# Loading two small parameter vectors from GpSimd and reading a branch flag at two moments, in a fused attention and rational MLP kernel

## The chip, the cores and the metric

The kernel runs on one core of one Trainium2 chip. The metric is the device time of one execution in microseconds (us). Before the change it is 251.97 us, the median of three runs (251.5 to 252.45).

## The reference

Linear attention with a sketched product kernel is followed by an MLP with a rational activation. Inputs are `q`, `k`, `v` of shape (4, 4, 1088, 32), two sketches `S1`, `S2` (8 x 32), `w_in` (128 x 2048), `w_out` (2048 x 128), and two small vectors `a` (4 values) and `b` (2 values).

```python
def phi(x):
    a = np.einsum('rd,bhsd->bhsr', S1, x)
    b = np.einsum('rd,bhsd->bhsr', S2, x)
    return np.einsum('bhsi,bhsj->bhsij', a, b).reshape(*x.shape[:-1], r * r)
kv = np.einsum('bhsf,bhsd->bhfd', phi(k), v)
num = np.einsum('bhsf,bhfd->bhsd', phi(q), kv)
den = np.einsum('bhsf,bhf->bhs', phi(q), np.sum(phi(k), axis=2))[..., None] + 1e-06
# tokens: (4352, 128), the heads side by side
h = (num / den) @ w_in
P = a[0] + a[1]*h + a[2]*h**2 + a[3]*h**3
Q = 1.0 + np.abs(b[0])*np.abs(h) + np.abs(b[1])*h**2
out = (P / (Q + 1e-06)) @ w_out
```

Note that `P / Q` is a ratio of polynomials in `h`; `b` alone decides which form of it the kernel can use.

## The kernel before

**Two programs behind one branch.** `run` (L123) is built twice: with `Fast`, always executed, and with `General`, executed only if the flag `special` is set (L834 to L837). In this data the flag is 0, so the second body is jumped over. The flag is computed on GpSimd from `b`, and every engine loads it into a register (`flag`, L793) before the compare-and-branch at the end (its instructions carry L836).

**Order of the work.** Nothing is scheduled by a compiler: `ORDER` (L24) is a list of steps `name:index`, and each step issues its instructions in that order, each engine taking its own in sequence. The steps that matter here: `ba` takes the absolute value of `b` on ScalarE (L818) and then runs `fitting` (L757), 14 small instructions on GpSimd that produce the flag and `c_fit`; `bi` runs `factors` (L774), a reciprocal `c_inv` on VectorE (L775) followed by five small GpSimd instructions that make scale factors; `rg` loads some of them into ScalarE registers; `wo` scales `w_out` by the factors; `lq`, `lk`, `lv`, `lw`, `lx` issue loads from SyncE's queue; `st` stores a block of output; `fl` loads the flag; `hi` marks a place for the branch hint.

**The first attention block.** Keys of batch 0 (class `Keys`, L297) come in three parts: `kt` transposes k on VectorE (L315), `ks` multiplies by the sketches on TensorE (L323), `kc` copies one half out of PSUM on ScalarE (L330), `kf` forms the 64 products per row on VectorE (L335, buffer `k_p`), `kp` multiplies them with v on TensorE (L364), `kk` copies the result to `kvz` on ScalarE (L374). Queries of batch 0 come as blocks 0 to 3 (`qt` transpose on VectorE L387 into one of two `qT` buffers, `qs` sketches on TensorE L400 or L473, `qc` copy on ScalarE L407 or L410, `qf` products on VectorE L416 or L419, `qp` TensorE L428, `qd`, `qi`, `qx` denominator, reciprocal and quotient on VectorE L437, L444, L449, `qb` transpose on TensorE L455, `qk` copy on ScalarE L462 into `xT`). Blocks 0 and 1 use columns 0 to 511 of q, which are loaded first; blocks 2 and 3 use the rest, loaded by `lq:0`.

**The MLP.** For 17 units of 4096 columns `h` does the first matmul (L519) in four pieces, `e` copies each to bf16 on ScalarE (L525), further steps on ScalarE and VectorE build three terms, and `G` accumulates them against `w_out` (L677). `st` transposes 256 or 512 columns of the sum on VectorE into `out_sb` (L686) and stores them with four DMAs (L694), all from SyncE, but for the last block, where two of the four come from ScalarE's queue.

**Queues and semaphores.** Loads go out from SyncE and, at the very start, from ScalarE: `s_raw`, two pieces of k, then `a_sb` (L209) and `b_sb` (L211), each broadcast to 128 partitions. Eight semaphores serve the DMAs of these two queues in turn, so a DMA waits until the eighth DMA before it, in program order over both queues, has landed.

GpSimd's own program before the chain of `ba` is: the masks (L229 to L233, from which VectorE makes the sketch matrices at L255), memsets, the identity, and copies `S21` and `SAB` of the sketches (L261, L267).

Of the kernel before, what the change touches and what calls it, by code (L numbers as in the profile page):

```python
# [19 lines left out]
class Fast:  # L20
# [1 line left out]
    R_ON_ACT = (0, 0, 0, 0, 1, 1, 0, 0, 1, 0, 0, 0, 0, 1, 1, 1, 0, 0, 0, 0, 0, 1, 0, 0, 0, 0, 1, 0, 0, 0, 1, 1, 1, 1)  # L22
    TURNS = (11, 0, 0, 0, 2, 0, 0, 0, 0)
    ORDER = """  # L24
tn:4 tn:0 lw:1 lq:0 kt0:0 lw:0 kt1:0 lx:1 kt2:0 lx:0 ks1:0 kt3:0 ks0:0 lk:1 qt:0 ks2:0 kc0:0 kc1:0 kf0:0 kf1:0 qs:0
kc2:0 qt:1 kf2:0 qc:0 kp0:0 ba:0 kp1:0 qf:0 kp2:0 qt:3 qs:1 kk:0 bi:0 qt:2 lq:1 lv:1 qc:1 qf:1 qp:0 qd:0 qs:2 qi:0
qx:0 qb:0 wo:3 qc:2 qk:0 qf:2 wo:0 qp:1 qs:3 qp:2 qd:1 wo:5 wo:1 h2:0 qd:2 wo:4 e2:0 qi:1 h3:0 qx:1 qi:2 h0:0 wo:2
qx:2 qb:1 rg:0 kt0:1 e3:0 e0:0 qb:2 pd1:0 qk:2 h1:0 kt1:1 u1:0 m1:0 lk:2 qk:1 e1:0 qc:3 ks0:1 ks1:1 qt:6 qt:4 h2:1
pd0:0 u0:0 kc0:1 kc1:1 kf0:1 m0:0 kt0:2 ln1:0 h0:1 e2:1 kt1:2 ex1:0 e0:1 v0:0 rd1:0 h1:1 ks1:2 qs:4 kf1:1 h3:1 qt:5
# [24 lines left out]
G1:14 h3:16 m1:14 u0:16 x1:14 ra1:15 ln0:16 e2:16 ex0:16 e3:16 s1:15 u2:16 m1:15 G0:14 u3:16 G5:14 G1:15 G0:15 G3:14  # L54
ra0:16 ln3:16 G2:14 ln2:16 G4:14 G0:16 ex3:16 pd1:15 s0:16 x1:15 G3:15 ex2:16 st:14 m0:16 ra3:16 ra2:16 s3:16 pa0:16
G4:15 G5:15 pa2:16 pa3:16 s2:16 G6:16 hi:0 m3:16 G1:16 G4:16 G2:15 m2:16 G3:16 G7:16 x0:16 st:15 G2:16 x2:16 G5:16
x3:16 G8:16 fl:0 st:16
    """.split()
    W_ENG = (1, 1, 0, 0, 0, 1)
    P_ON_ACT = (0, 0, 0, 0, 0, 0, 0, 0, 0, 0, 0, 0, 0, 0, 0, 0, 0, 0, 0, 0, 0, 0, 0, 0, 0, 0, 0, 0, 0, 0, 0, 0, 1, 1)  # L60
# [62 lines left out]
def run(  # L123
# [13 lines left out]
    nc = tc.nc  # L137
    ctx = ExitStack()
    fast = plan.FAST
# [15 lines left out]
    consts = ctx.enter_context(tc.tile_pool(name="consts", bufs=1))  # L155
# [38 lines left out]
    for i, s_in in enumerate((S1, S2)):  # L194
# [5 lines left out]
                      in_=bass.AP(tensor=k.tensor, offset=k.offset, ap=[[S * D // 32, 128], [W, NM], [1, 4 * D]]))  # L200
    nc.sync.dma_start(out=k0[:, 0:km].rearrange("p (m x) -> p m x", m=NM - 1)[:, :, 4 * D:],
                        in_=k0_src[:, 0:km].rearrange("p (m x) -> p m x", m=NM - 1)[:, :, 4 * D:])
# [3 lines left out]
    nc.sync.dma_start(out=q0[:, 0:512], in_=q0_src[:, 0:512])  # L206
    a_sb = consts.tile([128, 4], FP, name="a_sb")
    b_sb = consts.tile([128, 2], FP, name="b_sb")
    nc.scalar.dma_start(out=a_sb, in_=bass.AP(tensor=moe_a.tensor, offset=moe_a.offset,  # L209
                                              ap=[[0, 128]] + list(moe_a.ap)))  # L210
    nc.scalar.dma_start(out=b_sb, in_=bass.AP(tensor=moe_b.tensor, offset=moe_b.offset,  # L211
                                              ap=[[0, 128]] + list(moe_b.ap)))
    nc.scalar.preload_act_table_set("abs_reciprocal_sqrt_and_small" if fast else "natural_log_exp_and_others")
    load_v(0)
# [7 lines left out]
    def turn(i, cols=512):  # L222
        idle_ps = bank()
        for _ in range(plan.TURNS[i]):
            nc.tensor.matmul(idle_ps[:, :cols], lhsT=idle[:, 0:128], rhs=idle[:, :cols], start=True, stop=True)
# [48 lines left out]
    b_fit, c_fit, c_inv = (consts.tile([128, 2], FP, name=x) for x in ("b_fit", "c_fit", "c_inv"))  # L274
    a_k = consts.tile([128, 3], FP, name="a_k")
    special = consts.tile([128, 1], mybir.dt.int32, name="special")
    k_in_reg, k_sq_reg = (nc.scalar.alloc_register(x) if fast else None for x in ("k_in_reg", "k_sq_reg"))
    a1, a2, a3 = a_sb[:, 1:2], a_sb[:, 2:3], a_sb[:, 3:4]
    a3_reg = nc.scalar.alloc_register("a3_reg" if fast else "a3_reg_g")
# [401 lines left out]
    def store(i):  # L681
        t0, tl, f0, per = units[i]
        if f0 + per < nf:
            return
        o = mid.tile([128, TC], FP, name="out_sb")
        nc.vector.transpose(out=o[:, :tl], in_=outs[t0][:, :tl])  # L686
        c = t0
        while c < t0 + tl:
            b = c // S
            ce = min(t0 + tl, (b + 1) * S)  # L690
            o_b = out[b * S:(b + 1) * S, :].rearrange("(g j) d -> g j d", g=32)
            j0, j1 = (c - b * S) // 32, (ce - b * S) // 32
            for e in range(d_model // 32):
                (nc.scalar if t0 + tl == n_tok and e % 2 else nc.sync).dma_start(  # L694
                    out=o_b[:, j0:j1, e * 32:(e + 1) * 32],
                    in_=o[e * 32:(e + 1) * 32, c - t0:ce - t0].rearrange("p (j d) -> p j d", d=32))
            c = ce
# [8 lines left out]
    def w_part(x):  # L706
        y, f = x // 2, x % 2 * (nf // 2)
        o, t = w_sb[y][:, f:f + nf // 2], w_out_sb_f[:, f:f + nf // 2]
        if fast:
            if plan.W_ENG[x]:  # L710
                nc.scalar.activation(out=o, in_=t, func=ACT.Copy, scale=a_k[:, y:y + 1])
            else:
                nc.vector.tensor_scalar(out=o, in0=t, scalar1=a_k[:, y:y + 1], scalar2=None, op0=AX.mult)
        elif y == 2:
            (nc.scalar.copy if plan.W_ENG[x] else nc.vector.tensor_copy)(out=o, in_=t)
        elif plan.W_ENG[x]:
            nc.scalar.activation(out=o, in_=t, func=ACT.Copy, scale=a_sb[:, y:y + 1])
        else:
            nc.vector.tensor_scalar(out=o, in0=t, scalar1=a_sb[:, y:y + 1], scalar2=None, op0=AX.mult)
# [37 lines left out]
    def fitting():  # L757
        g = nc.gpsimd
        g.tensor_mul(out=sq, in0=ab0, in1=ab0)
        by(lim, ab1, AX.mult, 2.0 ** -10)  # L760
        by(fit, ab1, AX.is_ge, 2.0 ** -20)
        by(b4, ab1, AX.mult, 2.0)
        by(fit, ab1, AX.is_le, 2.0 ** 20, AX.mult, fit)
        by(fit, ab0, AX.is_ge, lim, AX.mult, fit)
        by(fit, b4, AX.is_ge, sq, AX.mult, fit)
        by(lim, fit, AX.mult, -1.0, AX.add, 1.0)
        by(b_fit, b_abs, AX.mult, fit, AX.add, lim)
        by(b4, b_fit[:, 1:2], AX.mult, 4.0)
        g.tensor_mul(out=sq, in0=b_fit[:, 0:1], in1=b_fit[:, 0:1])
        g.tensor_copy(out=special, in_=lim)  # L770
        by(c_fit[:, 1:2], b4, AX.mult, 1.0 + 1e-6, AX.subtract, sq)
        g.tensor_copy(out=c_fit[:, 0:1], in_=b_fit[:, 0:1])
# [12 lines left out]
        if any(plan.P_ON_ACT):  # L785
            nc.scalar.reg_load(a3_reg, a_sb[0:1, 3:4].bitcast(mybir.dt.int32))

    value = []

    def hint():  # L790
        tc.mark_branch_hint_location("special", "LikelyTaken", [mybir.EngineType.PE, mybir.EngineType.DVE, mybir.EngineType.Activation, mybir.EngineType.SP])

    def flag():  # L793
        value.append(nc.values_load(special[0:1, :], min_val=0, max_val=1, skip_runtime_bounds_check_because="a comparison gives 0 or 1"))

    does = {"e": evac, "h": hidden, "u": d_abs, "w": d_w, "y": d_y, "ln": a_square if fast else a_ln, "ex": a_root if fast else a_exp, "ra": a_inv, "rd": d_inv, "pa": a_p, "pd": d_p,
            "s": d_s, "m": d_hs, "v": d_v, "x": d_g, "G": gather}
# [6 lines left out]
    for step in plan.ORDER:  # L804
        name, i = step.split(":")
        i = int(i)
        if name in q_does:
            getattr(blocks[i](), q_does[name])()
        elif name in k_does:
            getattr(keys[i](), k_does[name][0])(*k_does[name][1:])  # L810
        elif name == "wo":
            w_part(i)
        elif name in loads:
            fetched[name, i] = loads[name](i)
        elif name == "tn":
            turn(i)
        elif name == "ba":
            nc.scalar.activation(out=b_abs, in_=b_sb, func=ACT.Abs)  # L818
            if fast:
                fitting()  # L820
            else:
                nc.scalar.reg_load(a3_reg, a_sb[0:1, 3:4].bitcast(mybir.dt.int32))
        elif name in ("bi", "rg", "hi", "fl"):
            {"bi": factors, "rg": registers, "hi": hint, "fl": flag}[name]()
        elif name == "st":
            store(i)
        else:
            does[name[:-1]](i, int(name[-1]))
# [5 lines left out]
def kernel(tc, *args):  # L834
    special = run(tc, Fast, *args)
    with tc.If(special > 0, label="special"):  # L836
        run(tc, General, *args)  # L837
# [30 lines left out]
```

## Time and profile before

| | us |
|---|---|
| median of three runs | 251.97 |
| lowest, highest | 251.5, 252.45 |
| the profiled execution's own time | 251.9 |
| its span, first to last instruction | 250.0 |
| TensorE busy in it | 240.5 |
| VectorE busy | 233.0 |
| ScalarE busy | 227.9 |
| GpSimd busy | 7.5 |

The profile is of one execution. Its engines are called PE (TensorE matmuls), PEld (weight loads), DVE (VectorE), ACT (ScalarE), POOL (GpSimd) and SP (SyncE); a "q" behind a name means the engine's sequencer, which issues DMAs, waits and branches. Times in a row are the start from the span's beginning and the duration, in us. A row may merge several like instructions (x4), and ends with the idle time before it and what ended that wait. The granted TensorE clock was 0.998 over the span.

### The profile page before, as it was taken

What the parts mean: (1) busy time and instruction counts of PE and PEld (TensorE: products, weight loads), DVE (VectorE), ACT (ScalarE), POOL (GpSimd) and SP (SyncE); (2) the same over time, 40 slices, a digit from 0 to 9 for tenths busy, and PEclk for the clock granted to TensorE, in tenths of its full rate; (3) what the DMA queues carried; (4) which work ended last, traced back from release to release, by engine and by line L of the source; (5) the groups of instructions that cost most, each with busy time, mean ns of one, the idle gap of its engine ahead of it and who ended that gap; (6) DMA issues with size and microseconds to landing.
All of it is one profiled execution on the core that took longest, in us unless ns stands there. A gap on an engine that the chain in (4) does not pass through costs nothing.

```text
span 250.0 us, 4083 instructions
## 1 busy us (share of the span) xinstructions
PE 240.5 (96%) x1585; PEld 133.8 (54%) x1585; DVE 233.0 (93%) x233; ACT 227.9 (91%) x217; POOL 7.5 (3%) x43
## 2 busy tenths in 40 slices
PE   7889999999999999999999999999999999999990
PEld 2668546645645455445555344444544467666770
DVE  3776999899999999999999999999999999999990
ACT  2267999999999999999999999999999999999980
POOL 4340000000000000000000000000000000000000
PEclk9999999999999999999999999999999999999999
DMA  5995348464413176210512200030020211020032
GB/s 155 257 387 89 99 121 188 134 156 78 144 27 100 28 202 138 69 45 16 148 22 77 67 3 0 16 102 3 0 42 0 40 25 22 0 37 8 0 49 42
DMA packets 30534, 19.60 MB, mean 78 GB/s; under 512 B 20400, under 2 KB 26672, under 8 KB 30512
## 3 DMA queue, kind: packets, MB, share of 16 engines
q1 hardware_dynamic: 28864, 18.92, 30.4%
q10 hardware_dynamic: 1648, 0.40, 0.9%
q8 instruction: 13, 0.21, 0.4%
q14 instruction: 9, 0.07, 0.1%
HBM read 16.16 MB, written 3.15 MB: 77 GB/s over the span
## 4 chain that ended last, share of the span: by engine, by line
PE 77%; DVE 13%; DMA 3%; issue 3%; SPq 0%; DVEq 0%
PE h_ps L519 42%; PE att_ps L677 23%; PE att_ps L428 4%; DVE g L658 4%; PE att_ps L364 4%; DVE g L647 3%; DVE s L643 2%; DMA k_sb<-in_k_dram 2%; PE att_ps L455 2%; DMA v_sb<-in_v_dram 2%; PE att_ps L473 2%; PE att_ps L323 1%; DVE p L600 1%; DVE r L630 1%; DVE out_sb L686 1%
## 5 line engine op out<-in xcount | busy, mean ns | idle before, releaser
L519 PE MATMUL h_ps<-xT,w_in_sb 128*128 128x512 f32 (+1 forms) x320 | 125.8, 532 | 0.0
L519 PEld LDWEIGHTS h_ps<-xT,w_in_sb 128*128 128x128 f32 x320 | 59.3, 190 | 44.4 <-issue 34.0
L525 ACT CAST hh<-h_ps 128x1024 bf16<-128x1024 f32 x68 | 72.2, 1086 | 2.1 <-PE h_ps L519 1.9
L613 ACT ACTIVATE ln<-u 128x2048 f32<-128x2048 bf16 (+1 forms) x35 | 67.2, 1950 | 0.0
L677 PEld LDWEIGHTS <-w_out 128*128 128x128 bf16 x432 | 41.8, 98 | 46.0 <-issue 16.5
L618 ACT ACTIVATE r<-ln 128x2048 bf16<-128x2048 f32 x22 | 44.0, 2002 | 0.0
L643 DVE TENSOR_TENSOR s<-hh,r 128x4096 bf16<-128x4096 bf16 (+2 forms) x21 | 39.2, 1872 | 0.0
L677 PE MATMUL att_ps<-r,w_out 128*128 128x512 bf16 (+1 forms) x160 | 34.8, 347 | 0.1
L677 PE MATMUL att_ps<-g,w_out 128*128 128x512 bf16 (+1 forms) x160 | 34.4, 347 | 0.0
L647 DVE TENSOR_TENSOR g<-hh,s 128x4096 bf16<-128x4096 bf16 (+2 forms) x16 | 27.8, 1744 | 0.3 <-PE att_ps L677 0.3
L658 DVE TENSOR_TENSOR g<-g,p 128x4096 bf16<-128x4096 bf16 (+2 forms) x15 | 27.7, 1849 | 0.0
L630 DVE TENSOR_TENSOR r<-r 128x2048 bf16<-128x2048 bf16 x22 | 26.5, 1217 | 0.0
L677 PE MATMUL att_ps<-s,w_out 128*128 128x512 bf16 (+1 forms) x112 | 24.5, 349 | 0.4 <-DVE s L643 0.4
L618 ACT ACTIVATE ln<-ln 128x2048 f32<-128x2048 f32 (+1 forms) x13 | 24.4, 1895 | 0.0
L624 ACT ACTIVATE r<-ln 128x2048 bf16<-128x2048 f32 (+1 forms) x13 | 23.7, 1868 | 0.0
L600 DVE TENSOR_SCALAR p<-hh,a_sb 128x4096 bf16<-128x4096 bf16 (+1 forms) x17 | 21.6, 1273 | 0.6 <-ACT hh L525 0.6
L548 DVE TENSOR_SCALAR u<-hh 128x2048 uint16<-128x2048 uint16 (+2 forms) x24 | 21.7, 905 | 0.4 <-ACT hh L525 0.4
L647 DVE TENSOR_TENSOR g<-hh,p 128x2048 bf16<-128x2048 bf16 (+1 forms) x7 | 11.6, 1663 | 0.0
L658 DVE TENSOR_TENSOR g<-g,s 128x2048 bf16<-128x2048 bf16 (+1 forms) x8 | 11.6, 1463 | 0.0
L428 PEld LDWEIGHTS att_ps<-kvz,q_pT 128*64 128x64 f32 x288 | 9.8, 137 | 3.3 <-issue 1.7
L428 PE MATMUL att_ps<-kvz,q_pT 128*64 128x66 f32 x288 | 11.1, 224 | 0.0
L364 PE MATMUL att_ps<-v_sb,k_p 128*64 128x64 f32 (+1 forms) x288 | 9.2, 222 | 1.0 <-DMA v_sb<-in_v_dram 1.0
(79 smaller groups left out, 146.6 us busy)
## 6 DMA issues: line engine op xcount, KB each, us to landing
a_all<-sk_d SPq DMA_DIRECT2D x6, 384.0 KB
b_all<-sk_d SPq DMA_DIRECT2D x12, 192.0 KB
v_sb<-in_v_dram SPq DMA_DIRECT2D x12, 144.0 KB
k_sb<-in_k_dram SPq DMA_DIRECT2D x3, 544.0 KB
q_sb<-in_q_dram SPq DMA_DIRECT2D x3, 544.0 KB
a_all<-sk_d SPq DMA_DIRECT2D x4, 320.0 KB
b_all<-sk_d SPq DMA_DIRECT2D x8, 160.0 KB
w_out_sb_f<-in_moe_w_out_dram SPq DMA_DIRECT2D x2, 512.0 KB
```

The costliest lines, as they stand in the source:

```text
L428: nc.tensor.matmul(self.nd[g * 64:(g + 1) * 64, o:o + 2 * KW], lhsT=self.q_p[:, c, x + g * 64:x + (g + 1) * 64], rhs=kvz[self.b % 2][:, c, ...
L519: nc.tensor.matmul(t[:, x * tl:(x + 1) * tl], lhsT=w_in_sb[:, f * 128:(f + 1) * 128], rhs=xT[:, x_at(t0):x_at(t0) + tl], start=True, stop= ...
L525: nc.scalar.copy(out=live[i]["hh"][:, part * PW:(part + 1) * PW], in_=live[i]["h", part])
L600: nc.vector.tensor_scalar(out=part_of(i, "p", h), in0=hh, scalar1=a3, scalar2=a2, op0=AX.mult, op1=AX.add)
L613: nc.scalar.activation(out=t, in_=live[i]["u"][:, span(h)], func=ACT.Square, scale=k_in_reg, bias=1.0)
L618: nc.scalar.activation(out=t if r_on_act(i, h) else part_of(i, "r", h), in_=t, func=ACT.Abs_reciprocal_sqrt, scale=k_sq_reg, bias=1.0)
L624: nc.scalar.activation(out=part_of(i, "r", h), in_=live[i]["ln", h], func=ACT.Square)
L630: nc.vector.tensor_mul(out=t, in0=t, in1=t)
L643: nc.vector.tensor_mul(out=part_of(i, "s", h), in0=hh, in1=part_of(i, "r", h))
L647: nc.vector.tensor_mul(out=part_of(i, "g", h), in0=hh, in1=part_of(i, "p" if horner(i, first(h)) else "s", h))
L658: nc.vector.tensor_mul(out=g, in0=g, in1=part_of(i, "s" if horner(i, first(h)) else "p", h))
L677: nc.tensor.matmul(outs[t0][:, :tl], lhsT=w_sb[y][:, f0 + x, :], rhs=part_of(i, key, h)[:, c:c + tl], start=done[0] == 0, stop=done[0] == ...
```

## The change

Four edits, all in `run` and `Fast.ORDER`:

- `a_sb` and `b_sb` are loaded from GpSimd's queue, as its first two instructions ahead of the masks, and no longer from ScalarE's.
- `ba:0` moves from behind `kp0:0` to the third place, ahead of all other ScalarE compute. `bi:0` moves from behind `kk:0` to just behind `qf:0`, ahead of `kp2:0 qt:3 qs:1 kk:0 qt:2`.
- `kf2:0` (VectorE, L335) now stands ahead of `qt:1` (VectorE, L387).
- The flag: at `fl:0`, SyncE, ScalarE and GpSimd load it as before. TensorE and VectorE load it at a new last step `fm:0` from a copy, `late_special`, which GpSimd writes after a dummy copy that reads the last `out_sb`, so after the last output transpose.

```diff
-tn:4 tn:0 lw:1 lq:0 kt0:0 lw:0 kt1:0 lx:1 kt2:0 lx:0 ks1:0 kt3:0 ks0:0 lk:1 qt:0 ks2:0 kc0:0 kc1:0 kf0:0 kf1:0 qs:0
-kc2:0 qt:1 kf2:0 qc:0 kp0:0 ba:0 kp1:0 qf:0 kp2:0 qt:3 qs:1 kk:0 bi:0 qt:2 lq:1 lv:1 qc:1 qf:1 qp:0 qd:0 qs:2 qi:0
+tn:4 tn:0 ba:0 lw:1 lq:0 kt0:0 lw:0 kt1:0 lx:1 kt2:0 lx:0 ks1:0 kt3:0 ks0:0 lk:1 qt:0 ks2:0 kc0:0 kc1:0 kf0:0 kf1:0
+qs:0 kc2:0 kf2:0 qt:1 qc:0 kp0:0 kp1:0 qf:0 bi:0 kp2:0 qt:3 qs:1 kk:0 qt:2 lq:1 lv:1 qc:1 qf:1 qp:0 qd:0 qs:2 qi:0
...
-x3:16 G8:16 fl:0 st:16
+x3:16 G8:16 fl:0 st:16 fm:0
...
-    nc.scalar.dma_start(out=a_sb, in_=bass.AP(tensor=moe_a.tensor, offset=moe_a.offset,
+    nc.gpsimd.dma_start(out=a_sb, in_=bass.AP(tensor=moe_a.tensor, offset=moe_a.offset,
...
-    nc.scalar.dma_start(out=b_sb, in_=bass.AP(tensor=moe_b.tensor, offset=moe_b.offset,
+    nc.gpsimd.dma_start(out=b_sb, in_=bass.AP(tensor=moe_b.tensor, offset=moe_b.offset,
...
+    late_special = consts.tile([1, 1], mybir.dt.int32, name="late_special")
...
         o = mid.tile([128, TC], FP, name="out_sb")
+        last_out[:] = [o]
...
-    value = []
+    value, last_out = [], []
+    special_handles = nc.alloc_registers("special") if fast else None
+    special_regs = {h.engine: h for h in special_handles.handles} if fast else None
...
     def flag():
-        value.append(nc.values_load(special[0:1, :], min_val=0, max_val=1, skip_runtime_bounds_check_because="a comparison gives 0 or 1"))
+        for e in (nc.sync, nc.scalar, nc.gpsimd):
+            e.reg_load(special_regs[e.engine], special[0:1, :])
+
+    def late_flag():
+        nc.gpsimd.tensor_copy(out=late_special, in_=last_out[0][0:1, 0:1])
+        nc.gpsimd.tensor_copy(out=late_special, in_=special[0:1, :])
+        for e in (nc.tensor, nc.vector):
+            e.reg_load(special_regs[e.engine], late_special)
+        value.append(nc.snap(special_handles, min_val=0, max_val=1))
```

More of the change, by code (lines that the diff above doesn't have):

```diff
@@ L822, in run @@
                 nc.scalar.reg_load(a3_reg, a_sb[0:1, 3:4].bitcast(mybir.dt.int32))
-        elif name in ("bi", "rg", "hi", "fl"):
-            {"bi": factors, "rg": registers, "hi": hint, "fl": flag}[name]()
+        elif name in ("bi", "rg", "hi", "fl", "fm"):
+            {"bi": factors, "rg": registers, "hi": hint, "fl": flag, "fm": late_flag}[name]()
         elif name == "st":
```

## The prediction

> **What bounds the kernel now.** I read the page first, to see which engine has no room.
>
> ```profile
> PE 240.5 (96%) x1585; PEld 133.8 (54%) x1585; DVE 233.0 (93%) x233; ACT 227.9 (91%) x217; POOL 7.5 (3%) x43
> ```
>
> Three engines are over 90% busy, and none of their instructions is removed except two DMA issues. So the body between some 18 and 240 us can only be shifted, and the change must win or lose at the two ends. The second view is the chain of work that ended last, over the first 35 us (start, duration, what).
>
> ```profile
> 6.03 3.98 DMA v_sb<-in_v_dram
> ...
> 10.26 2.32 PE att_ps L364 x72
> 12.58 1.06 PE h_ps L400 x8
> 13.64 0.64 PE att_ps L428 x16
> ...
> 14.29 0.44 DVE qT L387
> ...
> 15.65 0.43 DVE x_tok L449
> ...
> 18.05 5.38 PE h_ps L519 x24
> ```
>
> The start hangs on a DMA (v lands at 6.03 + 3.98 = 10.01), then on PE, then at 14.29 on DVE, and from 18.05 PE runs the MLP without a gap. The hand-over to DVE is where the change acts. The timeline of DVE shows why it was late:
>
> ```profile
> 14.21 0.17 DVE L775 RECIPROCAL c_inv<-c_fit 128x2 f32<-128x2 f32 x1 [1.05 <-POOL c_fit L772]
> 14.29 0.44 DVE L387 STREAM_TRANSPOSE qT<-q_sb 128x256 f32<-128x256 f32 x1
> 14.66 0.65 DVE L416 TENSOR_TENSOR q_pT<-h_ps,a_all 128x512 f32<-128x512 f32 x1
> ```
>
> DVE sat idle for 1.05 us behind a reciprocal that waits for GpSimd, with a transpose queued behind it that PE needs.
>
> The other end is the timeline of the last store; DVE, ACT and SP have these rows:
>
> ```profile
> 244.14 0.45 DVE L686 STREAM_TRANSPOSE out_sb<-att_ps 128x256 f32<-128x256 f32 x1 [0.69 <-PE att_ps L677]
> ...
> 244.62 0.87 ACTq L694 DMA_DIRECT2D out_dram<-out_sb  x2
> 244.78 0.32 SPq L694 DMA_DIRECT2D out_dram<-out_sb  x1
> ...
> 245.14 2.01 SPq L694 DMA_DIRECT2D out_dram<-out_sb  x1
> ```
>
> Call T the end of the last transpose, 244.59. Four equal stores follow. Three take 0.32 to 0.46 us to issue (two together 0.87 on ACT); the fourth takes 2.01 and ends at 247.15, T + 2.56. The program's closing steps, by the instructions of L836 (duration in ns, first and last start):
>
> ```profile
> L836 SPq EVENT_SEMAPHORE  x8: 17/17/17, 247.8 to 248.6; - x8
> ...
> L836 PEldq COMPARE_BRANCH  x1: 396/396/396, 244.1 to 244.1; - x1
> L836 DVEq COMPARE_BRANCH  x1: 84/84/84, 244.2 to 244.2; - x1
> ...
> L836 ACTq COMPARE_BRANCH  x1: 76/76/76, 245.5 to 245.5; - x1
> L836 SPq COMPARE_BRANCH  x1: 70/70/70, 247.2 to 247.2; - x1
> ```
>
> SP branches when its fourth issue is done (247.2), clears eight semaphores until 248.6, and the span ends at 250.0. So the end is SP's fourth issue plus about 2.85 us. What held that issue? The DMA queues in the 0.2 us from 245.3 (the digits are 40 slices of 5 ns), then the one other slow store issue of this trace and the queues at that moment (0.2 us from 65.8):
>
> ```profile
> DMA  0000000090900000000000000000000000000016
> ...
> q8 instruction: 1, 0.02, 43.2%
> q14 instruction: 1, 0.01, 16.2%
> ```
>
> ```profile
> 65.86 1.32 SPq L694 DMA_DIRECT2D out_dram<-out_sb  x1
> ```
>
> ```profile
> q8 instruction: 1, 0.02, 30.0%
> ```
>
> Two instruction fetches start at 245.34 and 245.35, about 1.2 us after the branches of PE and DVE (244.1, 244.2). The larger one fills 43.2% of 16 engines x 0.2 us, so it holds one DMA engine for 1.38 us, to about 246.73. At 65.8 a fetch of the same queue (30.0% of 3.2 us = 0.96 us, to about 66.8) sat under another store, whose issue took 1.32 us and ended at 67.18. In both places the issue ends some 0.4 us after the fetch does. I read the 2.01 us as the fetch holding one DMA engine, and the store's issue waiting for room in that engine's queue.
>
> **The change part by part.** *The late flag (term 1).* PE and DVE now load the flag after two GpSimd copies that follow T. For their cost, two dependent GpSimd steps, and PE's register load:
>
> ```profile
> 11.51 0.37 POOL L755 TENSOR_SCALAR fit<-b_abs,lim,fit 128x1 f32<-128x1 f32 x1
> 11.97 0.36 POOL L755 TENSOR_SCALAR fit<-b,sq,fit 128x1 f32<-128x1 f32 x1
> ```
>
> ```profile
> L794 PEldq TENSOR_LOAD <-special x1: 490/490/490, 243.5 to 243.5; - x1
> ```
>
> Dependent steps follow each other by 0.46 us. First copy at T + 0.08, second at T + 0.54, done at about T + 0.75; load 0.49 to T + 1.25; branch at T + 1.35; fetch 1.2 us later, T + 2.55. Without a fetch the fourth store issues in 0.45: 245.14 to 245.59, T + 1.00, 1.56 us sooner. Its data then need what they needed before: in the 0.6 us from 247.5 (slices of 15 ns)
>
> ```profile
> DMA  0000000000334548689999899866542210000000
> ```
>
> the packets run from 247.65 to 248.0, 0.85 us past the issue's end. So the last store would be written at T + 1.85, before PE's fetch. ACT's fetch (branch at 245.5, T + 0.9, plus 1.1) comes at T + 2.0 and just misses too. SP's closing steps are not queued behind PE or DVE: those branch at T + 1.4 and are through by T + 2, and SP's semaphores would run from T + 1.7 to T + 2.4. Two more semaphores (the new queue has its own) cost some 0.1. Gain 1.45; bounds 0 (the issue stays at 2.01) and 1.56. I take 1.45.
>
> Here the Trainium skill speaks against the change. Its page "Runtime: NRT & Kernel Launch", section "Instruction fetch mechanics", says that a taken branch whose target is outside the two pages held makes the engine wait for a DMA fetch before it goes on. That is rival 1 below. The rows above show the reverse for SP: it branches at 247.2 and clears its first semaphore at 247.8, sooner than the 1.1 us that a fetch takes to start after a branch.
>
> *The reciprocal ahead (term 2).* With c_inv early, DVE's transpose for query block 2 waits for PE, as it writes a buffer that PE's L400 reads until 12.58 + 1.06 = 13.64. It runs 13.70 to 14.14, not from 14.29. The next DVE instruction, q_pT, then waits for this copy:
>
> ```profile
> 13.69 0.58 ACT L407 COPY a_all<-h_ps 128x512 f32<-128x512 f32 x1 [0.59 <-PE h_ps L400]
> ```
>
> ```profile
> 14.79 1.14 PE L400 MATMUL att_ps<-qT,SAB 64*128 64x256 f32 x8 [0.52 <-DVE qT L387]
> ```
>
> which ends at 14.27, so q_pT starts at 14.33, not 14.66. PE's sketches of block 2 start at 14.28 (PE is free then), not 14.79, and are no longer what DVE or PE waits for; x_tok comes 0.33 us sooner, and with it PE's transposes, copies and the MLP at 18.05. Gain 0.33, carried to T because PE, DVE and ACT are all shifted alike. Late next is ACT's copy. Bounds 0 and 0.52 (PE's whole wait).
>
> *Loads on GpSimd, absolute value first (cost 0).* No GpSimd DMA is in the trace. Two issues cost 0.9 us if they are as ACT's median store, 4.0 if as the slowest issue (2.01). I take 0.9 to 2, near the common rows. Behind them on GpSimd stand the masks that DVE needs before its first k transpose, and behind b's landing stands ACT's whole queue. The covers:
>
> ```profile
> 5.24 1.63 DVE L315 STREAM_TRANSPOSE kT<-k_sb 128x256 f32<-128x256 f32 x4 [1.50 <-DMA k_sb<-in_k_dram]
> ```
>
> ```profile
> 7.61 0.33 ACT L330 COPY b_sk<-att_ps 128x64 f32<-128x64 f32 x2 [2.64 <-PE att_ps L323]
> ...
> 9.74 0.21 ACT L818 ACTIVATE b_abs<-b_sb 128x2 f32<-128x2 f32 x1
> ```
>
> ```profile
> 10.03 0.19 POOL L759 TENSOR_TENSOR sq<-b_abs 128x1 f32<-128x1 f32 x1 [5.14 <-ACT b_abs L818]
> ...
> 13.99 0.18 POOL L772 COPY c_fit<-b_fit 128x1 f32<-128x1 f32 x1
> ```
>
> DVE is idle for 1.50 us ahead of 5.24, ACT idle until 7.61. The GpSimd chain takes 14.17 - 10.03 = 4.14 us. c_inv now stands behind q_pT of block 0, about 11.6, so b_abs must end by 7.4 for no wait at all, and by 8.3 for none that matters, since DVE's next instruction waits for q's second half until 12.65 anyway. Issued by 2 to 3 us and landing some 3 later, b is there by 6. ACT's own two issues, which go, stood in idle time. For GpSimd's loads the Trainium skill, page "DMA: Bandwidth & Descriptors", section on the anatomy of a DMA on the gpsimd path, gives a fixed cost of about 2.0 us each; by it, as an estimate, both end within 4 us, and the sum stays.
>
> *The loads of v, and k_p ahead of a transpose (taken at 0).* With two DMAs fewer in the rotation, the third and fourth load of v wait for landings at about 3 us instead of k's, and go out some 1.5 us sooner. But the DMA engines are full then:
>
> ```profile
> 6.00:8.00 2.00, 2.00 (x39) 1.20 (x37) 1.44 (x5) 0.33 (x2) 0.00 (x0) 1.00 1.07 224
> 8.00:10.00 2.00, 1.22 (x14) 0.70 (x10) 2.00 (x4) 0.98 (x3) 0.00 (x0) 1.00 0.77 182
> ```
>
> DMA share (the column before GB/s) is 1.07 from 6 to 8 us, so v's landing is a matter of bytes, and PE's 72 matmuls run from it in one piece; k_p's move does not show then. If v did land sooner (0.77 from 8 to 10 leaves room), PE could start at 9.2, and its last 40 of 72 matmuls would wait for k_p until about 10.6: 0.7 us gained. A loss here is at most the weight of two tiny loads, 0.15.
>
> *Sum*, against the profiled execution's 251.9 (span 250.0 plus 1.9 outside it; the median of the runs is 251.97): 251.9 - 1.45 - 0.33 = **250.1**.
>
> **Rivals.** 1: The late branch itself becomes the end. If PE must have its fetch before it can join the closing barrier, it is held from T + 2.55 for 1.38 us, joins at T + 4.1 instead of SP at T + 4.6 before: gain 0.5 and 0.33, 251.1. For it: nothing in this trace has a branch so late on PE. Against: SP's row above. 2: The 2.01 us is not the fetch but four stores of two queues at once; it stays, 251.6. Against: at 65.86 only one queue was storing. It also covers the case in which the change doesn't do what it says because another fetch takes that place. 3, slower: GpSimd's load of b is late and holds ACT's queue, and c_inv, now earlier in DVE's order, holds DVE. It decides at b_abs ending at 8.3 us; beyond that each us costs one. If each GpSimd issue takes 2.01 and b lands 6.5 after it (9.74 - 3.22 is the most that it took before), b_abs ends near 11.4, c_inv comes at 15.6 instead of 14.2, with three DVE instructions still behind it that now stand before: about 3.5 us lost, 251.9 - 1.8 + 3.5 = 253.6. Against: the small load has 16 engines and its own queue. 4: v lands sooner, 0.7 more: 249.4.
>
> **How the numbers follow.** Forecast 0.56 (249.7 to 250.6); rival 1 0.16, rival 2 0.11, rival 3 0.10, rival 4 0.07. Rivals 1 and 2 reach to 251.6, half of rival 4 lies above 249.5: the range 249.5 to 251.6 leaves rival 3 and the edges out. A measurement of this kernel can tell about 0.5% (1.26 us) from no change. Below 250.7: forecast, rival 4 and a quarter of rival 1, 0.67. Above 253.2: rival 3, 0.09. Between: 0.24.
>
> **What would show it.** Term 1: all four last stores issue in under 0.5 us, SP branches near T + 1, and the fetches after PE's branch lie behind the last store. Term 2: no idle time before c_inv; block 2's transpose right behind PE's L400; the first MLP matmul about 0.33 us sooner against v's landing. Wrong if an issue near the end still takes 1 us or more, if PE's or DVE's last instructions come after SP's, if ACT's first copy waits for b_abs, or if v lands at another time than 10.0.

## The result and the profile after

| | before | changed |
|---|---|---|
| median, us | 251.74 (5 runs, 251.31 to 252.45) | 253.88 (5 runs, 253.33 to 254.01) |
| ratio of the times | | 1.0086, 95% interval 1.0063 to 1.0108 |
| profiled execution: own time, span | 251.9, 250.0 | 253.33, 251.4 |
| T, end of the last output transpose | 244.59 | 245.04 |
| from T to the end of the span | 5.4 | 6.4 |

The change made the kernel 2.1 us slower; the forecast was 250.1 us, 1.8 us below the profiled execution's 251.9. In the profiled executions (the changed one is the fastest of its five) 0.45 us are lost up to T and 1.0 behind it. Line numbers after the change are larger by 1 to 12.

**The head.** The chain of work that ended last, first 20 us of the changed kernel (start, duration, what):

```profile
3.93 6.62 DMA v_sb<-in_v_dram
10.55 0.53 issue
11.08 2.32 PE att_ps L365 x72
13.40 1.09 PE h_ps L401 x8
...
18.57 1.49 PE h_ps L520 x6
```

The 72 matmuls with v start at 11.08 and not at 10.26: 0.82 us late. The MLP starts at 18.57 and not at 18.05: 0.52 late. So the new order gives 0.30 back in between. DVE's timeline shows how:

```profile
12.26 0.14 DVE L777 RECIPROCAL c_inv<-c_fit 128x2 f32<-128x2 f32 x1
12.97 0.51 DVE L388 STREAM_TRANSPOSE qT<-q_sb 128x320 f32<-128x320 f32 x1 [0.56 <-DMA q_sb<-in_q_dram]
14.51 0.45 DVE L388 STREAM_TRANSPOSE qT<-q_sb 128x256 f32<-128x256 f32 x1 [1.02 <-PE h_ps L401]
15.13 0.69 DVE L417 TENSOR_TENSOR q_pT<-h_ps,a_all 128x512 f32<-128x512 f32 x1 [0.17 <-ACT a_all L408]
```

The reciprocal waits for nothing, block 2's transpose waits for PE's L401 (which ends at 14.49), and q_pT for ACT's copy, as forecast. What is new is that everything from DRAM comes later. DVE's first work on k, and ACT's on b:

```profile
1.23 0.76 POOL L209 DMA_DIRECT2D a_sb<-in_moe_a_dram  x1 [0.80 <-POOLq L864]
...
6.32 1.51 DVE L316 STREAM_TRANSPOSE kT<-k_sb 128x256 f32<-128x256 f32 x4 [2.56 <-DMA k_sb<-in_k_dram]
...
7.26 0.20 ACT L830 ACTIVATE b_abs<-b_sb 128x2 f32<-128x2 f32 x1 [3.26 <-DMA b_sb<-in_moe_b_dram]
```

DVE waits for k until 6.32, where it started at 5.24. `b_abs` ends at 7.46 and holds nothing. The table of busy times by stretch tells where the time went (the last three columns are the granted clock, the DMA share and GB/s). Before:

```profile
3.00:4.00 1.00, 1.00 (x4) 0.39 (x3) 0.65 (x4) 0.31 (x1) 0.19 (x2) 1.00 0.87 176
4.00:5.00 1.00, 1.00 (x3) 0.30 (x2) 0.00 (x0) 0.97 (x1) 0.89 (x4) 1.00 1.05 324
```

Changed:

```profile
3.00:4.00 1.00, 1.00 (x4) 0.40 (x3) 0.65 (x4) 1.00 (x1) 0.87 (x10) 1.00 0.51 36
4.00:5.00 1.00, 1.00 (x7) 0.44 (x5) 0.00 (x0) 0.01 (x1) 0.92 (x5) 1.00 0.56 98
```

In these two us the DMA engines moved 134 KB and not 500 KB (GB/s times us), half idle, while the loads of k and q had been issued as early as before. This is a hole, not a crowd: the two small loads themselves are 0.2% of the 16 engines' time in the page's list of queues:

```profile
q0 software_dynamic: 64, 0.00, 0.2%
```

**The tail.** The last stores of the changed kernel:

```profile
245.07 0.87 ACTq L696 DMA_DIRECT2D out_dram<-out_sb  x2
...
245.23 0.82 SPq L696 DMA_DIRECT2D out_dram<-out_sb  x2
```

All four issue in under half a us, as forecast, and are out at 246.05 (T + 1.01). Then the closing steps, the instructions of L848 (duration in ns, first and last start):

```profile
L848 SPq EVENT_SEMAPHORE  x8: 17/17/17, 249.3 to 249.9; - x8
...
L848 DVEq COMPARE_BRANCH  x1: 84/84/84, 246.3 to 246.3; - x1
L848 PEldq COMPARE_BRANCH  x1: 402/402/402, 246.3 to 246.3; - x1
L848 SPq COMPARE_BRANCH  x1: 70/70/70, 246.5 to 246.5; - x1
L848 PEldq EVENT_SEMAPHORE  x1: 51/51/51, 246.8 to 246.8; - x1
L848 DVEq EVENT_SEMAPHORE  x1: 21/21/21, 246.9 to 246.9; - x1
```

PE and DVE go on half a us after their branches. SP branches at 246.5 and goes on at 249.3. SP's waits in this stretch (us in total, times, longest) say the same, in the changed kernel and then in the kernel before:

```profile
SPq L848 <- SPq L848: 2.7, 1, 2.7
```

```profile
SPq L836 <- SPq L836: 0.8, 2, 0.6
```

By the trace's semaphore events the last of the four stores had landed at 247.96, so in the changed kernel 1.3 us of that wait is for nothing that a semaphore tells. In the kernel before it is different: the stores landed at 247.81, 247.97, 248.13 and 248.36, and SP's semaphores follow at 247.83, 248.15 and 248.38. There SP's closing steps are waits for landings, and the landing of the last store sets the end.

### The profile page after: what moved, and what is told of

Its sections match the earlier page's. It is cut to its first block, busy times and chain, and to the rows that moved or that the text cites. A ratio compares the mean times of both kernels' runs of the same rounds, so it can differ in the third digit from the quotient of the medians.

```text
span 251.4 us, 4097 instructions
## 1 busy us (share of the span) xinstructions
PE 239.3 (95%) x1585; PEld 133.9 (53%) x1585; DVE 232.9 (93%) x233; ACT 228.0 (91%) x217; POOL 9.2 (4%) x47
## 3 DMA queue, kind: packets, MB, share of 16 engines
q1 hardware_dynamic: 28864, 18.92, 28.3%
## 4 chain that ended last, share of the span: by engine, by line
PE 41%; ACT 27%; DVE 17%; issue 7%; DMA 3%; SPq 1%; POOL 0%; DVEq 0%; ACTq 0%; POOLq 0%
PE h_ps L520 22%; PE att_ps L678 13%; ACT hh L526 8%; ACT ln L614 7%; DVE g L659 4%; DVE g L648 4%; ACT r L619 3%; ACT ln L619 3%; DVE s L644 3%; ACT r L625 3%; DMA v_sb<-in_v_dram 3%; DVE r L631 2%; PE att_ps L365 2%; PE att_ps L429 2%; DVE p L601 1%
```

## The experiments

Two losses had to be explained. For the tail: theory A, the place of SP's branch in its code makes SP wait (it stands just behind an edge, where one piece of SP's code ends and the next begins); B, the late branches do; C, GpSimd's queue with its own semaphores does. For the head: theory L, GpSimd's loads delay the transfers of k, q and v; M, the new order does (the early wait for b). Times are medians, each beside the kernel before measured on the same chip (251.72 to 251.93 us); ratios have their 95% interval, and as they are made from all runs they can differ from the ratio of the medians. The times of landings and of single instructions are the trace's own events.

**1. The late flag alone** (`late_flag_only`): the kernel before, with `late_flag`, `last_out` and the step `fm:0` of the change.

> The kernel before with the late flag alone (a, b and the order as before). SP's block gets one instruction more (the MOVE of the flag to its own register). Theory A (where SP's branch falls in the pages of code that SP holds decides): the four last stores issue in under 0.5 us each, SP branches near T + 1.5, but its first closing semaphore comes 2.7 us later and not 0.64; the end is T + 6.4 against T + 5.4 before, so 251.7 + 1.0 = 252.7 us. Theory B (the late branches of PE, DVE or GpSimd hold SP): the same 252.7. Theory C (the semaphores of GpSimd's own queue hold SP): that queue is not used here, so the end is about T + 4.3 and the time 250.6. The head is as before under all three: v lands at 10.0 and the first MLP matmul starts at 18.05.

252.52 us, ratio 1.0036 (1.0022 to 1.0050). The four stores issue in under 0.5 us; the last lands at T + 2.8 (T + 3.8 before); SP's first semaphore comes 2.73 us after its branch, 1.4 after the last landing. So the wait needs no GpSimd queue: theory C falls.

**2. One instruction more on SP** (`one_more_on_sp`), with a spare register:

```diff
-ex2:16 st:14 m0:16
+ex2:16 st:14 np:0 m0:16
+        elif name == "np":
+            nc.sync.reg_load(spare, special[0:1, :])
```

> The kernel before with one instruction added on SP, a register load of the flag into a register that nothing uses, between the stores of unit 14 and the last unit; the flag, its branches, a, b and the order as before. Theory A: SP's branch is moved one place on, into the next page of SP's code, as in the changed kernel; SP branches at about 247.2 as before, and its first closing semaphore comes some 2.7 us after it and not 0.64: 251.7 + 2.1 = 253.8 us. Theory B and theory C: a register load in SP's idle time costs nothing, 251.7.

253.08 us, 1.0063 (1.0042 to 1.0083). As nothing reads the register, the load becomes a single 17 ns semaphore instruction at 239.3, in idle time. Nothing else is changed, and SP's first closing semaphore moves to 249.33, 0.97 us after the last landing (248.36). In SP's rows its branch has not moved, but the eight semaphores behind it have (247.8 to 248.6 in the kernel before):

```profile
L839 SPq EVENT_SEMAPHORE  x8: 17/17/17, 249.3 to 249.9; - x8
...
L839 SPq COMPARE_BRANCH  x1: 70/70/70, 247.1 to 247.1; - x1
```

The span ends at T + 6.63 and not at T + 5.38: 1.25 us for one idle instruction (1.24 in the medians). Theory B (late branches) falls as the cause, and the size of 2.1 was too large because SP waits for landings until 248.38 in the kernel before anyway.

**3. The changed kernel with one instruction less** (`changed_one_less`):

```diff
-        value.append(nc.snap(special_handles, min_val=0, max_val=1))
+        value.append(nc.snap(special_handles, donate=True, min_val=0, max_val=1))
```

> The changed kernel, with the flag's register handed on as it is and not copied: one MOVE less on each engine, so that SP's branch is again at the place that it has in the kernel before; all else as changed. Theory A: SP branches near T + 1.5 and clears its first semaphore 0.64 us later; the end is T + 4.3 against T + 6.4, so 253.9 - 2.1 = 251.8 us, unless PE's or DVE's fetch after the branch is then what ends last (at most 0.5 more). Theory B (late branches) and theory C (GpSimd's queue): the wait of 2.7 us stays, 253.8.

251.54 us, 0.9993 (0.9980 to 1.0005): 2.3 us less than the changed kernel. SP's first semaphore stands 1.57 us behind its branch, which I first took for a smaller wait of the same kind. It is a landing: the store that it waits for landed at 247.47, the semaphore came at 247.49.

**4. The changed kernel with the early flag** (`changed_early_flag`): `flag` as before, so only the loads and the order are changed.

> The changed kernel with the flag loaded as before by all engines ahead of the last store: a, b on GpSimd and the new order alone. Head, all theories: T 0.45 us later than before, as in the changed kernel (v lands near 10.9, the first MLP matmul starts at 18.57). Tail by theory A and by theory B: as before, SP's fourth issue 2.0 us and the end at T + 5.4 (two more semaphores, 0.1): 251.7 + 0.5 = 252.2 to 252.3 us. Theory C: SP waits here too, 253.8 or more.

253.08 us, 1.0054 (1.0037 to 1.0072), 0.8 more than expected. No wait of the new kind is in it: the first semaphore comes at 250.23, the landing at 250.22. With the early flag the last store lands at T + 3.8 as in the kernel before, so this is the cost of the loads and the order. The profiled execution was the slowest of its eight (254.29): its first MLP matmul is 0.87 late (18.92), and it loses some 1.0 more between 56 and 75 us, for which I have no cause.

**5. The loads alone** (`loads_on_gpsimd`): the kernel before, `nc.scalar.dma_start` of a and b as `nc.gpsimd.dma_start`.

> The kernel before with a and b loaded by GpSimd, nothing else changed (old order, early flag). Theory L (GpSimd's two small loads delay the landings of k, q and v at the start): v lands at 10.3 to 10.9 us, not at 10.0, and the first MLP matmul starts some 0.8 later, 18.7 to 18.9; with the old order the whole delay is carried to T. Rival M (what came later in the changed kernel came from the early wait for b on ACT or from the new order, not from the loads): v lands at 10.0 and the matmul starts at 18.05. Tail: SP's branch stands at the same place as before, but so it did with the changed kernel's early flag, where SP waited 1.59 us behind its branch and not 0.64. If GpSimd's queue brings that wait, it is here too. Time by L with that wait: 251.8 + 0.8 + 0.95 + 0.1 = 253.6; by L without it 252.7; by M 251.8 to 252.9.

253.49 us, 1.0076 (1.0062 to 1.0090). The same hole (35 and 104 GB/s in the two us from 3 to 5), the first MLP matmul at 19.28 in the chain (18.05 before). With the old order the delay does more harm: `b_abs` stands behind ACT's copy for query block 0, whose q came late, so it starts at 10.94 and not at 9.74, and the chain of factors ends last:

```profile
15.43 0.17 DVE L775 RECIPROCAL c_inv<-c_fit 128x2 f32<-128x2 f32 x1 [1.00 <-POOL c_fit L772]
```

Theory L holds, rival M falls. The extra wait behind SP's branch (2.70 us) is again a landing (249.52, semaphore at 249.53).

**6. The reciprocal behind the transpose** (`reciprocal_behind`): `bi:0 qt:2` to `qt:2 bi:0`, nothing else.

> The kernel before with one swap in the order: the reciprocal c_inv behind the transpose of query block 2, not ahead of it. Term 2 says that the transpose then starts when PE's L400 has ended (about 13.7 and not 14.29), the reciprocal runs in DVE's wait for ACT's copy, and the first MLP matmul starts 7.75 us after v's landing and not 8.04: 0.29 us sooner, 251.55. Rival: DVE then waits for c_fit as before, or another engine is late by as much, and the matmul stays 8.04 behind v's landing: 251.8.

251.56 us, 0.9987 (0.9976 to 0.9998). DVE's rows in its trace:

```profile
13.74 0.45 DVE L387 STREAM_TRANSPOSE qT<-q_sb 128x256 f32<-128x256 f32 x1 [0.56 <-PE h_ps L400]
14.11 0.14 DVE L775 RECIPROCAL c_inv<-c_fit 128x2 f32<-128x2 f32 x1
14.36 0.69 DVE L416 TENSOR_TENSOR q_pT<-h_ps,a_all 128x512 f32<-128x512 f32 x1
```

The MLP starts 7.74 behind v's landing (10.06 to 17.80) and not 8.04: 0.30, as expected.

**7. The changed kernel, SP's branch earlier still** (`changed_two_less`): as 3, and one store of the first unit from GpSimd.

> The changed kernel with the flag's register handed on and not copied (one instruction less per engine), and one of the four stores of the first unit, at 65 us, issued by GpSimd in place of SP: SP's branch stands one place earlier still. Theory A, if GpSimd's queue only moves SP's code by a place or two against its pages: the wait behind SP's branch goes from 1.57 to 0.64 us, and 251.5 becomes 250.6. Theory C (GpSimd's queue itself makes the wait of 1.57): it stays, 251.5.

251.73 us, 1.0005 (0.9994 to 1.0016). A miss, by the misreading of 3: the first semaphore now comes 0.89 us behind the branch, as it waits for another store, but the last landing is at T + 2.9 (T + 2.8 in 3) and the span ends at T + 5.0 (T + 4.8 in 3). It says that one place is enough.

**8. The late flag, the register handed on, and the swap of 6** (`late_flag_and_swap`), a and b on ACT.

> The kernel before with the late flag (its register handed on and not copied, so that SP's branch keeps its place) and the reciprocal behind the transpose; a and b on ACT. Theory A: the four last stores issue in under 0.5 us, SP branches near T + 1.5 and clears its first semaphore 0.64 later, the end is T + 3.7 against T + 5.4 before: 1.7 sooner, and 0.3 from the reciprocal, 249.8 us. Theory B (branches that come late hold SP): a wait of 1.6 or more behind SP's branch, 250.8 or more.

250.23 us, 0.9939 (0.9924 to 0.9954): faster than both kernels. SP's rows of L848:

```profile
L848 SPq EVENT_SEMAPHORE  x8: 17/17/17, 245.7 to 247.1; - x8
...
L848 SPq COMPARE_BRANCH  x1: 70/70/70, 245.2 to 245.2; - x1
```

T is 244.12; the four stores land by T + 2.76 (before T + 3.77), the last semaphores follow, and the span ends at T + 4.4 (before T + 5.4). I had expected T + 3.7, again without the landings.

**9. Twenty instructions more on SP** (`twenty_more_on_sp`): as 2, twenty times.

> The kernel before with twenty register loads of the flag added on SP between the stores of unit 14 and the last unit (SP is idle there), where one cost 1.25 us: the edge in SP's code that the branch then sat on is crossed some 20 us before the branch. Theory A1 (SP waits because the next page of its code is still being fetched when it branches): by the time of the branch that fetch is long done; SP's first closing semaphores come with the landings of the last stores, as before, 251.8 us. Theory A2 (crossing the edge throws out the branch's target, fetched ahead at the start, and it must be fetched again after the branch): SP's first semaphore comes over 1 us after the last landing, 252.8 to 253.3.

252.14 us, 1.0000 (0.9987 to 1.0014). A1 holds: twenty cost nothing where one cost 1.25 us. The twenty run back to back, and there the edge itself can be seen. The instructions of the added line in the stretches from 239.8 to 240.6 and from 240.6 to 241.7:

```profile
L828 SPq EVENT_SEMAPHORE  x10: 17/17/17, 239.9 to 240.6; - x10
```

```profile
L828 SPq EVENT_SEMAPHORE  x10: 17/17/17, 241.0 to 241.6; - x10
```

They follow each other by 0.06 to 0.10 us, but between the tenth and the eleventh (240.57 and 241.01) lie 0.44 us, and 0.67 us later an instruction fetch of 8 KB starts that the kernel before does not have. The DMA queues from 241 to 243 us:

```profile
q14 instruction: 1, 0.01, 1.3%
```

In order of time the tenth is SP's 207th instruction. In the kernel before the 207th is the branch; with one more instruction ahead of it the branch is the 208th, the first behind the edge. (The edge was crossed 5 us ahead of the branch, not 20 as I had written: these instructions stand behind the stores of unit 14, which SP issued from 237.9 to 239.9.)

**10. The loads on GpSimd, later** (`loads_on_gpsimd_late`): behind the identity, issued at 2.60 and 3.38 us, after k's and q's.

> The kernel before with a and b loaded by GpSimd, but issued behind its masks and the identity, at some 3 to 4 us and not at 1.2. With the issue at 1.2 us the DMA engines were busy for 9.0 and 8.0 us of 16 in the third and fourth us (14.0 and 16.9 in the kernel before). Theory L (GpSimd's own descriptors hold the DMA engines for some 2 us): the hole moves with the issue to some 5 to 7 us, k lands earlier than in the other run, v is late all the same, the first MLP matmul starts at 18.7 to 19.2 us and not 18.0; 252.5 to 253.5. Rival (the hole comes from the start, where the queues are empty, and not from GpSimd's descriptors): no hole, v at 10.0, 251.8.

252.79 us, 1.0042 (1.0023 to 1.0061), the runs from 251.98 to 254.1. From 3 to 5 us the DMA engines work as before (0.86, 1.06); from 6 to 8 their share is 0.97 and 0.95 (1.02 and 1.12 before), which is no hole like the other. Half of L: the harm is less when k and q are ahead of GpSimd's loads. The profiled execution (252.46, among the fastest) has its first MLP matmul at 18.16, only 0.11 late, and T and the last landing (T + 3.75) where they were. Its span is longer by 0.56 all the same, and that lies behind the last landing: the span ends 2.15 us after it, and not 1.61.

This third cost is in every kernel that uses GpSimd's queue. Leaving out the three in which SP stands still, the span ends 1.60 to 1.61 us after the last landing in the six profiles without a load on GpSimd, and 1.93 to 2.15 us after it in the seven with one. 0.12 to 0.25 of it is more to close behind SP's eighth semaphore, as SP's rows there show, in the kernel before and in `loads_on_gpsimd`:

```profile
L863 SPq EVENT_SEMAPHORE  x10: 17/28/28, 248.7 to 249.9; - x10
```

```profile
L863 SPq EVENT_SEMAPHORE  x12: 17/28/28, 250.2 to 251.6; - x12
```

The rest is order: in the kernel before the store that lands last is the fifth of SP's eight waits, here it is the first, and seven more follow it at 0.06 to 0.11 us each.

**11. With the key features ahead, too** (`late_flag_swap_kf2`): as 8, and `qt:1 kf2:0` to `kf2:0 qt:1`.

> As late_flag_and_swap (late flag, the register handed on, the reciprocal behind the transpose, a and b on ACT), with the key features kf2 ahead of the query transpose qt:1 too. The prediction took that move at 0, at most 0.7 if v lands early and k_p is what PE's matmuls of v wait for. By it: 250.2 as without the move. Rival (k_p is late and DVE's transpose can wait): up to 0.3 sooner, 249.9, with the first MLP matmul less than 7.75 us behind v's landing; or the query features are later by 0.4 and it is 250.6.

250.45 us, 0.9948 (0.9925 to 0.9970): not to be told from 8. The move is worth nothing that can be measured.

**12. The whole change without the loads on GpSimd and with the register handed on** (`no_gpsimd_loads`).

> The change without its two faults as I see them: the whole new order and the late flag, but a and b loaded by ACT as before, and the flag's register handed on and not copied. If these two are all that was lost (the loads on GpSimd about 0.8 to 1.2 us, the wait of SP behind its branch about 1.5), the time is 250.2 us, as of late_flag_and_swap. Rival: ACT's early wait for b, which now stands ahead of all its copies, costs time by itself where b comes by ACT's queue behind k; then b_abs ends at 8 us or later, b_sk's first copy (7.61 before) is late by as much, and the time is 250.7 or more.

250.65 us, 0.9953 (0.9933 to 0.9972). The intervals of 8, 11 and 12 overlap, so the early wait for b on ACT shows no clear cost in the time. Its mechanism is in the trace, though: `b_abs` runs from 7.95 to 8.15, ACT's first copy stands right behind it, and PE's last 40 matmuls with v wait for k_p until 11.03, at the end of that chain.

**13. The changed kernel with twenty instructions more on SP** (`changed_twenty_on_sp`), the copied register kept.

> The changed kernel as it is, the copy of the flag's register (MOVE) on each engine included, with twenty register loads of the flag added on SP between the stores of unit 14 and the last unit. Theory A1 (SP waits because it comes to an edge of its code just ahead of its branch, whatever instruction brought it there): the edge is crossed 20 us before; SP's first closing semaphores come with the landings, near T + 2.9, and the time is 251.6 to 252.4, though 20 instructions were added. Theory B2 (the MOVE on the engines, the late branches, or GpSimd's queue with either makes the wait): it stays at 253.8.

251.73 us, 1.0004 (0.9993 to 1.0015): 2.15 us less than the changed kernel, with more instructions. SP's rows:

```profile
L852 SPq EVENT_SEMAPHORE  x8: 17/17/17, 246.5 to 248.1; - x8
...
L852 SPq COMPARE_BRANCH  x1: 70/70/70, 246.0 to 246.0; - x1
```

The same gap of 0.44 us stands between its 207th and 208th instruction (240.21 and 240.65). The copy, the late branches and GpSimd's queue are all still there, and the wait is gone: B2 falls.

**14. Only b on GpSimd** (`only_b_on_gpsimd`).

> The kernel before with b alone loaded by GpSimd; a stays on ACT. With both on GpSimd the DMA engines were busy 0.56 and 0.50 of the time from 3 to 5 us (0.87 and 1.05 before), and the time was 1.77 us longer. Theory L1 (each small load on GpSimd holds the engines while its descriptors are made and read): b's load, now GpSimd's first instruction of its kind, makes half the hole, the share from 3 to 5 us is near 0.55 for one us and not two, the time 252.6 to 252.9. Theory L2 (the first use of GpSimd's queue makes the hole, whatever is loaded): the same hole as with both, 253.3 to 253.6. If the hole is gone, neither holds.

253.38 us, 1.0068 (1.0041 to 1.0095): one load costs 1.6 us, with two it was 1.8. The hole is as deep as with two:

```profile
3.00:4.00 1.00, 1.00 (x4) 0.40 (x3) 0.54 (x4) 0.79 (x1) 0.85 (x6) 1.00 0.30 8
4.00:5.00 1.00, 1.00 (x4) 0.30 (x2) 0.11 (x1) 0.49 (x1) 0.82 (x4) 1.00 0.71 68
```

L2 holds: one load on GpSimd's queue makes the hole, and a second adds little. In the profile 1.26 us of the cost are there at T, and the closing steps have theirs (experiment 10). In the changed kernel, where a is GpSimd's first load (issued at 1.23 us, ahead of k), a lands at 5.25 and k's pieces from 6.3 on.

## Why the prediction was wrong

The sum of the parts, from pairs of runs that differ in one of them: the new order and the late flag together -1.28 (12 against its before; of it the late flag -1.33, by 8 against 6, and the reciprocal -0.16 in the medians and -0.30 in the trace, by 6); the loads on GpSimd +0.98 under the new order (3, 0.30 below its before, against 12, 1.28 below its own) and +1.8 under the old (5); SP's branch one place on +2.15 (13) to +2.34 (3). Together +1.85 to +2.04; measured +2.14. That they add up is no proof: the runs 12, 3 and the changed kernel differ by one step each, so with +2.34 the sum closes by itself but for the 0.1 us between the chips. The loads' share holds the closing steps of experiment 10 (0.35 in this pair of profiles), and SP's wait is 1.6 in the profiles (T + 6.4 against T + 4.8 in 3), less than in the medians.

- *Term 1, the fourth store's issue.* Right: with the late flag all four issue in under 0.5 us in every kernel that has it, and the last store lands 1.0 us sooner against T. Its size, 1.45, was a little large (1.33 in the medians, 1.0 in the profiles): the stores need until T + 2.8, not T + 1.85, and SP waits for them. The slow issue is not the whole of it. In `twenty_more_on_sp` and `loads_on_gpsimd`, with the early flag, all four stores issue in under 0.5 us too, and the last landing is at T + 3.84 and T + 3.89 all the same. A store's semaphore rises in 16 steps: in `twenty_more_on_sp` 14 steps of the last store come by 247.68, the 15th at 248.14 and the 16th at 249.06, with a fetch of 8 KB from 245.96 to 246.56 and one of 16 KB from 246.24 to 247.36 ahead of them. In `late_flag_and_swap` the 16 KB start at 246.43, and all 16 steps of each of the first two stores come within 0.21 us. That fits fetches that hold a DMA engine; no run tests it by itself.
- *Term 1, SP's closing steps: the first failed step.* "SP's semaphores would run from T + 1.7 to T + 2.4. Two more semaphores ... cost some 0.1." They ran from T + 4.25. The sum has no term for the copied register, which puts one more instruction ahead of SP's branch. The branch thereby becomes the first instruction behind an edge in SP's code, and SP stands still after it until 1.3 us past the last landing. The new queue's semaphores cost 0.3 to 0.5 (experiment 10), and not 0.1.
- *The row that I used against rival 1.* That SP cleared its first semaphore 0.64 us after its branch was no proof that it needed no fetch; it was the landing of a store. The Trainium skill, page "Runtime: NRT & Kernel Launch", section "Instruction fetch mechanics", has taken branches wait for a fetch when their target is outside the pages held. The traces agree in that SP stands still for 2.2 to 2.75 us behind such a branch in three kernels, but PE, DVE, ACT and GpSimd take the same branch and go on within 0.6 us in every run here, and SP too (0.52 to 0.59 where no landing was late), unless its branch is first behind the edge. (SP, ACT, DVE and PE have a branch hint in the trace at 0.7 to 0.8 us, GpSimd has none and goes on as soon; no run leaves the hints out.) Rival 1 had put the wait on PE, and only PE.
- *Term 2, the reciprocal.* Right in mechanism and size (0.33 forecast, 0.30 in both traces).
- *Loads on GpSimd, cost 0: the second failed step.* What I counted came as forecast: the issues took 0.76 and 0.55 us, the masks were not late, `b_abs` ended at 7.46 where 7.4 to 8.3 was allowed. But b landed at 7.24 and not by 6: the two loads took 4.0 and 5.2 us from issue to landing, more than the 3 I had assumed. The estimate of 2.0 us each, by which both end within 4 us, is not borne out either. What I left out is what a load on GpSimd does to the transfers issued behind it on other queues: "A loss here is at most the weight of two tiny loads, 0.15." The weight was small, the loss 0.82 us at the first matmuls of v, of which the new order wins 0.30 back. The condition for being wrong that came true is the last: v landed at another time than 10.0.
- *Loads of v sooner, k_p ahead: 0.* v's last two loads went out 1.3 us sooner, as forecast, and gained nothing; the move of k_p is worth nothing (11).
- *Rival 3* gave 253.6, near the time, with a cause that did not happen: b was in time, and c_inv waited for nothing.

**What stays open.** What SP waits for behind the edge is not in the trace: of the instruction fetches that follow the branches the last of 8 KB is over by 248.0 and PE's of 16 KB by 248.9, no packet of any kind starts between 247.9 and 250.1, and SP goes on at 249.3. One mark of the edge is there: in the three kernels in which SP stands still a fetch of 8 KB starts 0.63 us behind SP's branch, as one does behind the edge in straight code (0.67 and 0.62 in 9 and 13), and in the other 13 profiles none starts from 0.6 to 0.95 us behind it. Shown is only that the place of the branch decides. Why GpSimd's first load leaves the DMA engines idle is open too; that the transfers issued behind it wait for its descriptors fits the order of landings and experiment 10, and was not tested further.

## What to carry to other kernels

Ask of each DMA that is moved to another queue what it stands ahead of: a load of 1 KB (b, 2 values to 128 partitions) cost 1.6 us, most of it because the large loads were issued behind it. Ask, too, what a queue that was not used before adds to the closing steps: here 0.3 to 0.5 us. Look, before pricing the end of a program, at which semaphores the closing instructions wait for and when those were given: a gap behind a branch can be a landing. And where an edit adds an instruction to an engine that nothing waits for, try the same edit with some more idle instructions, or one fewer, before crediting or blaming its mechanism.

## What the runs showed of the hardware

- One 17 ns instruction on SP cost 1.25 us, and twenty cost none: the place of a branch in an engine's code can be worth 0.5% of this kernel.
- In two runs SP paused for 0.44 us between two like instructions where it crossed an edge in its code, 5 us ahead of its branch.
- A load of 2 values to 128 partitions, issued by GpSimd at 1.2 us ahead of the loads of k, q and v from other queues, left the DMA engines at 0.30 and 0.71 of their time in two us in which they were at 0.87 and 1.05 without it.
- The span ended 1.60 to 1.61 us after the last store's landing in six profiles without a load on GpSimd's queue, and 1.93 to 2.15 us after it in seven with one.
- Of the 16 steps of the last store's semaphore 14 came by 247.68 and the other two 0.5 and 1.4 us later, where instruction fetches of 8 and 16 KB had run while the store was under way (`twenty_more_on_sp`).
